# Attention in groups of three units, with wider own maxima, a third q/k set and one sum step per pair, in a fused attention and two-expert-layer kernel

## The chip, the cores and the metric

The kernel runs on one core of one Trainium2 chip. The metric is the device time of one execution in microseconds (us), median of three runs. Engines are named as in the profile: PE (TensorE matmuls), PEld (weight loads of TensorE), DVE (VectorE), ACT (ScalarE), POOL (GpSimd), SP (the queue that issues the DMAs).

## The reference

Three layers in a row, all in float32. q, k and v are (4, 8, 1152, 64), so there are 32 heads.

```python
q_pool = q.reshape(B, H, S // 2, 2, D).mean(axis=3)      # 576 queries per head
scores = (q_pool @ k^T) / 8;  scores -= max over keys
attn   = exp(scores) / (sum over keys + 1e-9);  x = attn @ v   # to (2304, 512)
h = x @ w_in;  g = where(h > 0, h, exp(min(h, 0)) - 1);  x = g @ w_out   # d_ff 2048
logits = x @ phi;  d = softmax over tokens;  c = softmax over 32 slots
slots  = d^T x;  each of 8 experts: relu(slots @ w1[e]) @ w2[e];  out = c @ slot_out
```

## The kernel before

**Who orders the work.** Every step is given to `Plan.add` with a due time, an engine (or a choice of engines) and a duration. `Plan.run` plays the list through once with those durations, latencies (`lat`), a price for a change of TensorE's tiling (`SWITCH`, `HYST`) and priorities (`PRI`, `BIAS`, `LOOK`), and writes the instructions of each engine in the order that comes out. On the chip every engine works through its own list in that fixed order and waits on semaphores. Steps of the attention on TensorE (`fixed=True`) keep the order of their due times.

**Attention (phase 0).** Heads go in 16 pairs, the two heads of a pair side by side in 64 rows each. A pair has 18 units: two halves of 288 queries by nine blocks of 128 keys. A unit (`step`) is: `qk` on TensorE (L688), eight matmuls in 64-row tiles (mode "R") that give the scores less the row maximum in one of three PSUM tokens `psS` (two banks each); one exponential on ACT (L700) into an E tile in SBUF; `acc`, the running sum of the exponentials over the key blocks, on POOL or DVE (L709); and `pv` (L695), the product with v in 64-column tiles (mode "C") into the PSUM bank `psC[h]` of its half. There are six E tiles. Units go in groups of `GU = 2`: first the two `qk` of a group, then the two `pv` of the group before.

**The maxima.** The maximum over keys is needed before a pair's first exponential, so it is worked out one pair ahead from a single product: 576 queries in five tiles by 1152 keys. Six "own" steps per pair take 384 keys each (`max_unit`: `max_mm` L619 into a `psS` token, `max_red` L628 on DVE). The other cells, 192 keys each, are "carried": each of 18 units has one, written behind its scores in the same token and reduced by DVE after the unit's exponential. `max_end` gathers them per half with a small reduce (L668), a transposing product into `psC[h]` (L664) and two scalings (L672) into `nm`.

**Preparing a pair.** q and k are loaded by SP (L520), q is added in twos (`pool_q`, L562, on DVE or POOL). `prep_q` transposes six blocks (L580) through a `psS` token, `prep_k` transposes six blocks (L603) through a `psS` token and three through `psC[1]`. Each is then split into a rounded high part (ACT, L588 and L610) and a low part (DVE, L589 and L611). There are two sets of these operands, taken in turn.

**The sums.** After the last unit of each half a step of its own (`sums`, L719) adds the 128 partial sums with a product with ones in 64-column tiles; ACT writes it to `SS` (L722). After the second half `norm` sends `SS` through two small DMAs (`memf<-memf`) to 18 rows, DVE takes the reciprocal (L744), a DMA writes it to DRAM (`rscr`), two more spread it over the partitions, and a product (L749) gives x.

**After the attention.** The weights of the first expert layer are decoded on DVE during both phases (32 pieces, `decode`, L494 to L506). The layer itself (phase 1) is 32 slots of 48 matmuls for h (L856) and 48 for the output (L895); its first slots are mixed with the last pair of the attention. The last layer (phase 2) streams w1 and w2.

Of the kernel before, what the change touches and what calls it, by code (L numbers as in the profile page):

```python
# [8 lines left out]
F32 = mybir.dt.float32  # L9
# [38 lines left out]
SWITCH = 0.18  # L48


class Plan:
# [57 lines left out]
    def lat(self, a, b):  # L109
        if a == b:  # L110
            return 0.0 if a in ("PE", "SP") else 0.09
        if a == "PE":
            return 0.24
        if b == "PE":
            return 0.27 if a == "ACT" else 0.25
        return 0.16
# [135 lines left out]
PRI = {'1AtaPE': -5.3608, '1LTDVE': -0.4594, '1RTDVE': -7.6429, '2SO*': -0.4526, '1MSACT': -0.9307, '1DN*': 8.8491, '2DNACT': 0.2194, '1wph*': -4.7823, '2BePE': -2.9011, '2erSP': -2.9653, '1EmACT': 4.7478, '1wih*': -3.2155, '1SIDVE': -16.5066, '2yqSP': 2.4557, '1Llg*': -8.1331, '2GPool': 3.2101, '2GDVE': -7.1, '2CDVE': 4.4865, '1PH*': 6.0485, '1xn*': -2.6051, '2SELDVE': 3.5395, '2MDVE': -0.6846, '1xl*': 0.61, '1scroSP': 1.1261, '1DRDVE': -0.4279, '2SOP*': -4.7028, '1xnDVE': 0.4531, '2SIZDVE': 6.7579, '1PHDVE': -0.095, '1Lm*': 5.0157, '2zqSP': -4.2858, '2BsitPE': -5.2295, '1BlgPE': 2.9402, '1X*': -1.2546, '2BsoPE': -9.6495, '1BtaPE': 4.0529, '1MSDVE': -5.9118, '2SODVE': 2.4582, '1wil*': -1.2109, '2AePE': -1.6771, '2SIZPool': -1.8218, '2CPE': 0.3788, 'PMXDVE': 5.8326, '0zSP': 5.8562, '0phiSP': 2.4789, '0UA*': -0.3377, 'PnmACT': 7.2492, '0ONERPool': 2.0662, '0qhACT': 0.8522, '0TMPDVE': -0.5015, 'PKRSP': 2.8555, '0QRSP': 2.4444, 'PMZDVE': 0.1661, '0khACT': 3.538, '0RAWACT': -0.5107, '0ACC*': 1.3624, 'PNQDVE': -2.7745, '0SMSP': 1.1984, '0rscrSP': -1.2373, '0scriSP': -4.5893, '0RBSP': 3.284, 'PqhACT': -3.9283, '0NQ*': 0.8442, '0qlDVE': -4.8402, '0KRSP': -0.8079, '0EAACT': 1.6723, 'PkhACT': 4.0482, '0nmACT': 1.1685, '1AhPE': -5.4283, '1wjh*': -0.2497, '1xh*': -9.449, '1woh*': -13.1407, '1wjl*': 1.9459, '1Hlg*': 1.9084, '1Hm*': -1.551, '1XN*': 1.3572, '1scriSP': -0.3405, '1SI*': 5.0824, '1AoPE': -3.7062, '1LT*': -1.0977}  # L252
BIAS = [{'DVE': 2.6845, 'Pool': 1.8955, 'ACT': -0.4027}, {'DVE': -3.2955, 'Pool': 5.8552, 'ACT': -4.78}, {'DVE': 7.9625, 'Pool': 25.9664, 'ACT': 7.8882}, {'ACT': -14.3311, 'Pool': 2.7731, 'DVE': -2.1432}]
LOOK = {'PE': 0.0215, 'ACT': 0.293, 'DVE': 0.1477, 'Pool': 0.3598, 'SP': 5.2367}
STEP = 1.47
GU = 2
NDEC = [0, 0, 0, 0, 1, 0, 1, 1, 0, 0, 0, 0, 1, 0, 0, 1]
DECS = 0.7438
# [4 lines left out]
TM2 = [-14.582, 27.792, 22.6349, 17.3721]  # L263
TDT = [0.625, 1.728, 6.6355, 1.2]
WARM = [24]
OFF = {'wi': -10.8492, 'wo': 0.9719, 'h': -0.5713, 'o': -0.4908}
EP = 1.3
SLOT = 14.8061
EAV = [26.8636, 30.7913, 35.1115]
OGRP = [[2, 6, 12, 18], [6, 12, 16, 18]]  # L270
DQ = [-10, 0.61]
DK = [[-9, 0.3], [-9, 0.3]]
UC = -14
MAX1 = [[-2, 0.4], [-2, 1.3], [0, -0.1], [0, 0.9], [1, -0.1], [1, 1.3]]
# [12 lines left out]
def attention_moe_softmoe(  # L287
# [20 lines left out]
    MW, NM = 192, S // 192  # L308
# [40 lines left out]
    plan.rot["EA"] = plan.rot["E"] + plan.rot["U"]  # L349
# [7 lines left out]
    def bank(tok):  # L357
# [7 lines left out]
    BASE = {"r": 0, "f": 100000, "y": 200000, "z": 300000, "v": 400000}  # L365
    y_es, z_es = ctx.enter_context(ExitStack()), ctx.enter_context(ExitStack())
# [48 lines left out]
    MZ = carve("v", "MZ", 1, len(NT5) * D)[0].rearrange("p (a j m) -> p a j m", j=2, m=D // 2)
# [113 lines left out]
    for i in range(2):  # L529
        nc.gpsimd.memset(r32(qkb["nm", i]), 0.0)  # L530
# [856 lines left out]
```

## Time and profile before

| what | value |
|---|---|
| runs | 991.01, 995.22, 989.75 us; median 991.01 us |
| profiled execution | span 990.1 us from first to last instruction (no time of it is given beside the span; the median of the runs is 0.9 us above) |
| PE busy | 955.2 us (96%) |
| DVE, ACT, POOL busy | 757.0, 497.7, 396.2 us |
| mean granted TensorE clock | 0.980 |

A busy PE is a modelled figure: matmuls are pipelined, so the starts of the instructions, and not their lengths, tell how fast PE advances. Times in the rows are us from the span's start. fp32 matmuls show as two records each, so one `pv` (two matmuls) is four records of L695, a `qk` is eight of L688 (fp32r).

### The profile page before, as it was taken

The numbers are of one execution on the slowest core, as the hardware profiler recorded it, in microseconds if no ns is written. First come the engines' busy times: TensorE is split into PE (matmuls) and PEld (weight loads), VectorE is DVE, ScalarE is ACT, GpSimd is POOL, SyncE is SP. The second block draws the span as 40 slices with busy tenths as digits, with TensorE's granted clock in tenths as the row PEclk, the third lists the DMA queues.
The fourth block names the chain that finished last, engine by engine and source line by source line (L and its number), as shares of the span: only waits on it lengthen the run. The fifth ranks groups of instructions, "written<-read, shape, count | busy, mean of one in ns | idle before, by whom it ended". The sixth has DMA issues, their size and how long they took to land.

```text
span 990.1 us, 20893 instructions
## 1 busy us (share of the span) xinstructions
PE 955.2 (96%) x8474; PEld 782.5 (79%) x8474; DVE 757.0 (76%) x1278; ACT 497.7 (50%) x891; POOL 396.2 (40%) x278
## 2 busy tenths in 40 slices
PE   7999999999999999999999999999999999999885
PEld 4777767676777677677899999999999999998343
DVE  6677788888777778899998989998866877766213
ACT  2556566555665556565664444444434376442213
POOL 2878889798878878887400000000000000001000
PEclk7999999999999999999999999999999999999897
DMA  7133424224334322221263333333423023233999
GB/s 177 45 86 85 106 74 122 67 78 119 86 85 117 74 73 75 63 72 34 65 219 113 117 95 131 106 98 110 157 86 107 32 97 107 65 107 109 402 362 317
DMA packets 103663, 114.86 MB, mean 116 GB/s; under 512 B 43664, under 2 KB 74896, under 8 KB 103568
## 3 DMA queue, kind: packets, MB, share of 16 engines
q1 hardware_dynamic: 103568, 113.55, 37.7%
q8 instruction: 66, 1.08, 0.5%
q14 instruction: 29, 0.24, 0.1%
HBM read 100.27 MB, written 13.18 MB: 115 GB/s over the span
## 4 chain that ended last, share of the span: by engine, by line
PE 85%; DVE 8%; DMA 3%; ACT 1%; issue 1%; SPq 0%; ACTq 0%; DVEq 0%
PE psC L895 20%; PE psA L856 20%; PE psC L695 13%; PE psA L688 10%; PE psS L688 5%; PE psA L619 3%; PE psS L619 2%; DVE memf L628 2%; DMA memzq<-in_moe_w_dram 2%; PE psA L1241 2%; PE psC L719 1%; PE psA L603 1%; DMA memf<-memf 1%; PE psA L580 1%; PE psC L664 1%; PE psC L1277 1%
## 5 line engine op out<-in xcount | busy, mean ns | idle before, releaser
L709 POOL TENSOR_TENSOR memf<-memf 128x576 f32<-128x576 f32 x241 | 359.8, 1495 | 65.0 <-ACT memf L700 38.6
L895 PE MATMUL psC<-memz 128*128 128x288 f32 x1512 | 224.6, 296 | 1.2 <-DVE memf L906 0.7
L895 PEld LDWEIGHTS psC<-memz 128*128 128x128 f32 x1512 | 208.1, 188 | 4.6 <-ACT memf L514 1.6
L695 PE MATMUL psC<-memf 128*64 128x288 f32 x1152 | 174.6, 420 | 0.0
L700 ACT ACTIVATE memf<-psA 128x576 f32<-128x576 f32 x206 | 132.8, 651 | 66.8 <-PE psA L619 57.7
L628 DVE TENSOR_REDUCE memf<-psA 128x2 f32<-128x384 f32 (+3 forms) x235 | 142.4, 617 | 28.7 <-PE psA L619 13.9
L1347 POOL MEMSET memf<- 128x2048 f32 x1 | 1.8, 1817 | 387.8 <-DVE memz L517 387.8
L906 DVE TENSOR_TENSOR memf<-psC,memf 128x288 f32<-128x288 f32 x220 | 100.3, 462 | 47.4 <-PE psC L895 45.6
L628 DVE TENSOR_REDUCE memf<-psS 128x4 f32<-128x768 f32 (+1 forms) x140 | 103.5, 739 | 38.1 <-PE psS L619 21.2
L514 ACT CAST memz<-memf 128x576 fp32r<-128x576 f32 (+1 forms) x94 | 69.2, 749 | 82.6 <-PE psC L895 42.1
L695 PEld LDWEIGHTS psC<-memf 128*64 128x64 f32 x1152 | 70.0, 136 | 48.9 <-issue 9.9
L517 DVE TENSOR_TENSOR memz<-memf,memz 128x576 fp32r<-128x576 f32 (+1 forms) x108 | 96.9, 906 | 9.8 <-ACT memz L514 8.6
L856 PE MATMUL psA<-memz 128*128 128x288 f32 x512 | 93.8, 295 | 0.0
L867 ACT ACTIVATE memf<-psA 128x576 f32<-128x576 f32 x64 | 41.7, 652 | 103.3 <-PE psA L856 103.2
L688 PE MATMUL psA<-memr 64*128 64x288 f32 x816 | 73.3, 303 | 3.9 <-DVE memf L628 3.9
L856 PEld LDWEIGHTS psA<-memz 128*128 128x128 f32 x512 | 76.6, 188 | 0.0
L700 ACT ACTIVATE memf<-psS 128x576 f32<-128x576 f32 x82 | 53.4, 651 | 41.0 <-PE psS L619 36.1
L688 PEld LDWEIGHTS psA<-memr 64*128 64x128 f32 x816 | 60.1, 188 | 11.0 <-DVE memf L628 6.1
L688 PE MATMUL psA<-memy 64*128 64x288 f32 x624 | 61.3, 301 | 0.5 <-DVE memf L628 0.4
L856 PE MATMUL psA<-memz,memv 128*128 128x288 f32 x256 | 51.9, 296 | 0.0
L688 PEld LDWEIGHTS psA<-memy 64*128 64x128 f32 x624 | 47.3, 187 | 4.5 <-issue 3.5
L870 DVE SCALAR_TENSOR_TENSOR memf<-memf,psA 128x576 f32<-128x576 f32 x64 | 47.6, 744 | 1.7 <-ACT memf L868 1.6
(210 smaller groups left out, 1512.6 us busy)
## 6 DMA issues: line engine op xcount, KB each, us to landing
memf<-wscr SPq DMA_DIRECT2D x32, 512.0 KB
memzq<-in_moe_w_dram SPq DMA_DIRECT2D x30, 512.0 KB
memf<-in_moe_w_dram SPq DMA_DIRECT2D x26, 512.0 KB
memz<-in_q_dram SPq DMA_DIRECT2D x32, 288.0 KB
memz<-in_k_dram SPq DMA_DIRECT2D x32, 288.0 KB
memf<-in_v_dram SPq DMA_DIRECT2D x16, 576.0 KB
memf<-in_moe_w_in_dram SPq DMA_DIRECT2D x32, 256.0 KB
wscr<-memf SPq DMA_DIRECT2D x32, 256.0 KB
```

The costliest lines, as they stand in the source:

```text
L514: return lambda e: nc.scalar.copy(out_, in_) if e == "ACT" else nc.vector.tensor_copy(out_, in_)
L517: return lambda e: ENG[e].tensor_tensor(out_, a, b, ALU.subtract)
L619: nc.tensor.matmul(tile_[:m, j, lo : lo + n * MW], lhsT=qkb["qh", i][js, o : o + m], rhs=qkb["kh", i][js, g * MW : (g + n) * MW], start=Tr ...
L628: add(t, "DVE", dve(2 * n * MW), lambda: nc.vector.reduce_max(MX[i][:m, a, :, g : g + n], v4(got(psS, tok)[:m, :, lo : lo + n * MW], n), a ...
L688: nc.tensor.matmul(sp[:, j, :NH], lhsT=qkb[w, i][js, cs] if w else ONER[js], rhs=qkb[m, i][js, hs], start=(x == 0), stop=(x == 3))
L695: nc.tensor.matmul(psC[h][j * D : (j + 1) * D, :NH], lhsT=VR[i][:, j, c], rhs=e[:, j], start=(c == 0), stop=(c == NC - 1))
L700: add(t + 0.01, "ACT", act(NQ, True), lambda: nc.scalar.activation(got(EAf, E_), got(psS, S_)[:, :, :NH], AF.Exp, scale=1.0 / 16.0), r=[S_ ...
L709: ENG[e].tensor_tensor(ac, a, got(EAf, E_), ALU.add)
L856: nc.tensor.matmul(ph[:, t, :NH], lhsT=a, rhs=x, start=(i == 0), stop=(i == 3 * KD - 1))
L870: add(t + 1.2, "DVE", dve(NQ), lambda: nc.vector.scalar_tensor_tensor(got(Ef, uk), got(Uf, ek), -1.0, ph(), ALU.add, ALU.max), r=[ek, A], ...
L895: nc.tensor.matmul(po_(), lhsT=a, rhs=x, start=(i == 0), stop=(i == 3 * GF - 1))
L906: add(t0 + 0.8, "DVE", dve(NH), lambda: nc.vector.tensor_tensor(d, po_(), d, ALU.add), r=[ck], w=XK)
```

## The change

- Pair 0 keeps groups of two; pairs 1 to 15 go in six groups of three (`GS`). `LAG = 1`: only the last unit of a group has its `pv` in the next group's section; the `pv` of the others come in the group's own.
- Own maxima take 512 keys (six a pair, as before), and 13 carried cells of 212, 214 or 128 keys stand in place of 18 of 192. `CU` says which units carry: the second and third of each group, and unit 15.
- A third set of q/k operands (`qs(p)` in place of `p % 2`), and two KR tiles. From pair 1 on `part` transposes k in three pieces and q in two, all through `psC` in place of `psS`, almost two pairs ahead.
- One `sums` step a pair, with four products in 32-column tiles (two halves by two heads), one `SS` of 288 in place of 576 columns, four small DMAs to 36 rows in place of two to 18, and the reciprocal over 32 columns in place of 64. A third `ACC`.
- Eleven E tiles in place of six (`NEX = 5` more).
- The planner's durations and latencies of DVE and POOL, `SWITCH`, and the tables of priorities and due times are new. The attention's decodes go to other pairs (`NDEC`, six in place of five). q, k and the q sums are due at other times (`LQ`, `LK`, `LN`).

```diff
 def dve(n):
-    return n / 960 + 0.145
+    return n / 960 + 0.07
...
-    return n * 0.00229 + 0.11
+    return n * 0.00229 + 0.17
...
-SWITCH = 0.18
+SWITCH = 0.225
...
-            return 0.0 if a in ("PE", "SP") else 0.09
+            return 0.0 if a in ("PE", "SP") else 0.15 if a == "DVE" else 0.09
...
-GU = 2
-NDEC = [0, 0, 0, 0, 1, 0, 1, 1, 0, 0, 0, 0, 1, 0, 0, 1]
-DECS = 0.7438
+GS = [[2, 2, 2, 2, 2, 2, 2, 2, 2], [3, 3, 3, 3, 3, 3]]
+LAG = 1
+NDEC = [0, -1, 0, 0, 1, 0, -1, 1, 0, 1, 0, 0, 1, 0, 1, 1]
+DECS = 0.5808
...
-SLOT = 14.8061
+SLOT = 12.4951
...
+LQ = [-14.7, -13.9452, -17, -18]
+LK = [-16.5, -17.8646, -18, -22]
+CU = [1, 2, 4, 5, 7, 8, 10, 11, 13, 14, 16, 17, 15]
+PARTS = [..., ..., [['k', 0, -10, -0.1, 1], ['k', 1, -10, 1.7978, 1], ['k', 2, -9, 1.5042, 0], ['q', 0, -8, 1.5, 0], ['q', 1, -7, 1.6969, 0]]]
+MAX2 = [[-6, 1.6], [-5, 1.6], [-4, 1.5272], [-3, 1.6], [-2, 1.6], [-1, 1.6]]
...
-    plan.rot["EA"] = plan.rot["E"] + plan.rot["U"]
+    plan.rot["EA"] = plan.rot["E"] + plan.rot["U"] + [(f"EX{i}",) for i in range(NEX)]
...
+    def part(p, n, g, t, bk):
+        i = qs(p)
+        tok, own_ = ("C", bk), (f"piece{n}{g}", p)
+        m, w = (QC // 2, QP) if n == "q" else (NC // 3, P)
+        def tr():
+            for x in range(m):
+                src = NQt[:w, m * g + x] if n == "q" else KR[p % 2][:, m * g + x]
+                nc.tensor.transpose(psC[bk][:, x * w : (x + 1) * w], src.rearrange("p j d -> p (j d)"), ident[:w, :w])
+        ps = psC[bk][:, : m * w]
+        add(t, "PE", m * (0.092 if n == "k" else 0.08), tr, ...)
+        add(t + 0.01, "ACT", act(m * w, True), lambda: nc.scalar.copy(hi, ps), ...)
+        add(t + 0.02, "DVE", dve(m * w), lambda: nc.vector.tensor_tensor(lo, ps, r32(hi), ALU.subtract), ...)
...
+            whole = [(a, 0, 512, 0, 2) for a in range(5)] + [(4, 512, 512, 2, 2)]
+            part_ = [(a, lo, n, e, 1) for lo, n, e in ((512, 212, 2), (724, 214, 3), (938, 214, 4)) for a in range(3)]
+            part_ += [(3, 512, 212, 2, 1), (3, 724, 214, 3, 1), (3, 938, 214, 4, 1), (4, 1024, 128, 4, 1)]
...
-        t2 = TG(p, u // GU + 1, TC + 0.2 * (u % GU))
+        g2 = g + (k >= gs(p)[g] - LAG)
+        t2 = TP(p, g2, 0.2 * (k - (gs(p)[g] if g2 > g else 0)) + 0.2 * LAG)
...
-                for j in range(2):
-                    nc.tensor.matmul(psC[h][j * D : (j + 1) * D, :NH], lhsT=ONEF, rhs=ac[:, j], start=True, stop=True)
+                    for j in range(2):
+                        for x in range(2):
+                            o = (2 * j + x) * D // 2
+                            nc.tensor.matmul(psC[1][o : o + D // 2, :NH], lhsT=ONEF[:, : D // 2], rhs=accs[x][0][:, j], start=True, stop=True)
...
-        for j in range(2):
-            dma(t, SM[i][j * NC : (j + 1) * NC], SS[j * D : j * D + 1]..., [("SS", 0, 0), ("SS", 0, 1)], [("SM", i, j)], 5e3)
-        add(t + 2, "DVE", 0.55, lambda: nc.vector.reciprocal(rs, sm), ...)
+        for j in range(4):
+            dma(t, SM[i][j * NC : (j + 1) * NC], SS[j * D // 2 : j * D // 2 + 1]..., [("SS", 0)], [("SM", i, j)], 2.5e3)
+        add(t + 2, "DVE", 0.35, lambda: nc.vector.reciprocal(rs, sm), ...)
```

## Rows read from the trace of the kernel before

**Rows 1.** Stages: PE, PEld, DVE, ACT, POOL busy (count), clock, DMA share, GB/s.
```profile
57.02:452.00 394.98, 389.23 (x4089) 278.07 (x4087) 317.91 (x491) 236.41 (x415) 337.20 (x228) 1.00 0.33 84
...
502.87:897.99 395.12, 395.12 (x2965) 390.29 (x2965) 324.32 (x593) 182.54 (x309) 1.54 (x1) 1.00 0.32 105
...
897.99:990.10 92.11, 73.32 (x612) 40.03 (x612) 27.32 (x79) 21.56 (x67) 2.70 (x2) 0.88 0.89 314
```

**Rows 2.** Same view, two of the attention's pairs, between their last sum steps.
```profile
310.35:337.94 27.59, 27.59 (x295) 19.88 (x293) 22.41 (x37) 16.52 (x29) 23.56 (x17) 1.00 0.42 104
...
337.94:369.00 31.06, 29.39 (x295) 21.11 (x293) 21.64 (x37) 16.56 (x29) 23.31 (x17) 0.95 0.33 75
```

**Rows 3.** Timeline of PE inside one pair: start, duration, line, operands, count.
```profile
319.50 0.44 PE L619 MATMUL psS<-memr 64*128 64x384 f32 x2
...
319.78 0.58 PE L688 MATMUL psA<-memy 64*128 64x288 f32 x6
...
320.42 0.58 PE L688 MATMUL psA<-memy 64*128 64x288 f32 x6
...
321.15 1.19 PE L695 MATMUL psC<-memf 128*64 128x288 f32 x8
...
322.27 0.66 PE L688 MATMUL psS<-memy 64*128 64x288 f32 x6
...
322.90 0.25 PE L619 MATMUL psS<-memr 64*128 64x192 f32 x2
...
322.99 0.58 PE L688 MATMUL psA<-memy 64*128 64x288 f32 x6
...
323.72 0.71 PE L695 MATMUL psC<-memf 128*64 128x288 f32 x4
...
324.26 0.66 PE L719 MATMUL psC<-memf 128*64 128x288 f32 x4
...
324.74 0.66 PE L695 MATMUL psC<-memf 128*64 128x288 f32 x4
...
325.33 0.44 PE L619 MATMUL psA<-memr 64*128 64x384 f32 x2
```

**Rows 4.** Chain of waits near the transposes of one pair: start, length, what.
```profile
275.53 0.65 PE psA L580 x6
...
278.76 0.80 PE psA L603 x6
...
279.56 0.33 PE psC L603 x3
```

**Rows 5.** Chain of waits in the last stage, a matmul in four column groups.
```profile
926.42 15.71 PE psA L1241 x128
```

**Rows 6.** Timeline of DVE: two reduces, and a reciprocal that waited.
```profile
310.27 0.54 DVE L628 TENSOR_REDUCE memf<-psA 64x2 f32<-64x384 f32 x1
...
312.06 0.96 DVE L628 TENSOR_REDUCE memf<-psS 128x4 f32<-128x768 f32 x1 [0.43 <-PE psS L619]
...
345.42 0.54 DVE L744 RECIPROCAL memf<-memf 18x64 f32<-18x64 f32 x1 [2.41 <-DMA memf<-memf]
```

**Rows 7.** Waits of DVE from 28 to 452 us: total, times, longest.
```profile
DVE memf L744 <- DMA memf<-memf: 4.5, 3, 2.4
```

**Rows 8.** Timeline of the SP queue's DMA issues in pair 11.
```profile
335.57 2.73 SPq L520 DMA_DIRECT2D memz<-in_k_dram  x2
...
339.08 2.65 SPq L520 DMA_DIRECT2D memf<-memf  x2
```

**Rows 9.** Lines L709 and L562 by engine: min/median/max ns, first and last start.
```profile
L709 POOL TENSOR_TENSOR memf<-memf x241: 1395/1417/2296, 24.8 to 480.3; 128x576 f32<-128x576 f32 x121
...
L709 DVE TENSOR_TENSOR memf<-memf x15: 744/748/1980, 127.4 to 466.7; 128x576 f32<-128x576 f32 x15
...
L562 DVE TENSOR_TENSOR memf<-memz x13: 944/1452/2168, 5.4 to 390.5; 96x768 f32<-96x768 f32 x13
```

**Rows 10.** Costliest groups of the page: the exponential of a unit.
```profile
L700 ACT ACTIVATE memf<-psA 128x576 f32<-128x576 f32 x206 | 132.8, 651 | 66.8 <-PE psA L619 57.7
```

More of the change, by code (lines that the diff above doesn't have):

```diff
@@ L114, in lat @@
         if b == "PE":
-            return 0.27 if a == "ACT" else 0.25
-        return 0.16
+            return 0.27 if a == "ACT" else 0.32 if a == "DVE" else 0.25
+        return 0.235 if a == "DVE" else 0.16
     def run(self):
@@ L527, in attention_moe_softmoe @@
     nc.gpsimd.memset(MX[1], 0.0)
-    for i in range(2):
+    for i in (1, 0, 2):
         nc.gpsimd.memset(r32(qkb["nm", i]), 0.0)
@@ L618, in max_mm, with max_red @@
             js = slice(j * D, (j + 1) * D)
[L619 removed]
+            nc.tensor.matmul(tile_[:m, j, at : at + n], lhsT=qkb["qh", i][js, o : o + m], rhs=qkb["kh", i][js, lo : lo + n],
                              start=True, stop=True)
[L622 to L625 removed]
+    def max_red(tok, p, cell, at, t, behind=()):
@@ L626, in max_red @@
         i = p % 2
+        a, _, n, e, ne = cell
         m = QT[a][1]
-        add(t, "DVE", dve(2 * n * MW), lambda: nc.vector.reduce_max(
-            MX[i][:m, a, :, g : g + n], v4(got(psS, tok)[:m, :, lo : lo + n * MW], n), axis=AX.X), r=[tok, *behind], w=[("MX", i, a, g)])
-    def max_deps(p, g, n):
-        return [("qh", p % 2)] + [("kh", p % 2, x) for x in sorted({g // 4, (g + n - 1) // 4})]
-    def max_unit(p, a, g, t):
-        tok = ("S", "max", p, a, g)
-        add(t, "PE", 0.172, lambda: max_mm(got(psS, tok), p, a, g, 2, 0), r=max_deps(p, g, 2), w=[tok], mode="R", fixed=True)
-        max_red(tok, p, a, g, 2, 0, t + 0.01)
@@ L639, in attention_moe_softmoe, with max_deps @@
-    carry, own = {}, {}
+        add(t, "DVE", dve(2 * n), lambda: nc.vector.reduce_max(
+            MX[i][:m, a, :, e : e + ne], got(psS, tok)[:m, :, at : at + n].rearrange("p j (g k) -> p j g k", g=ne), axis=AX.X),
+            r=[tok, *behind], w=[("MX", p, a, e)])
+    def max_deps(p, cell):
+        a, lo, n = cell[:3]
+        qx, kx = ((0,), (0,), (0, 1), (1,), (1,))[a], range(lo // 384, (lo + n - 1) // 384 + 1)
+        return [("qh", qs(p), x) for x in qx] + [("kh", qs(p), x) for x in kx] + [("now", "qh", p, x) for x in qx] + [("now", "kh", p, x) for x in kx]
@@ L640, in attention_moe_softmoe, with max_unit @@
+    def max_unit(p, cell, t):
+        tok = ("S", "max", p, *cell[:2])
+        add(t, "PE", 0.012 + cell[2] / 2400, lambda: max_mm(got(psS, tok), p, cell, 0), r=max_deps(p, cell), w=[tok], mode="R", fixed=True)
+        max_red(tok, p, cell, 0, t + 0.01)
+    carry, own, cells_of = {}, {}, {}
     for p in range(NP):
-        own[p] = []
-        cells = {h: [(a, g) for a in ((0, 1, 2), (3, 4))[h] for g in range(0, NM, 2)] for h in range(2)}
         if p == 0:
-            own[p] = [(a, g, *((-7 + x // 2, 0.2 * (x % 2)) if GU == 2 else (-5 + x // 3, 0.2 * (x % 3)))) for x, (a, g) in enumerate(cells[0])]
-            own[p] += [(a, g, *MAX1[x]) for x, (a, g) in enumerate(cells[1])]
-            continue
@@ L647, in attention_moe_softmoe @@
-        for h in range(2):
-            nown = (4, 2)[h]
-            own[p] += [(a, g, *MAX2[h][x]) for x, (a, g) in enumerate(cells[h][:nown])]
-            units = [u for u in range(UC, UC + 18)][10 * h : 10 + 8 * h]
-            rest = sorted(((a, g + y) for a, g in cells[h][nown:] for y in range(2)), key=lambda x: x[1] // 4)
-            for u, x in zip(units, rest, strict=True):
-                carry[(p - (u < 0), u % NU)] = (p, *x)
-    cells_of = {(p, a, g) for p in own for a, g, *_ in own[p]} | set(carry.values())
+            whole = [(a, 384 * x, 384, 2 * x, 2 - x // 2) for a in range(5) for x in range(3)]
@@ L656, in max_end @@
+        cells_of[p] = {c[:1] + c[3:4] for c in whole + part_}
     def max_end(p, h, t):
@@ L687, in qk @@
                     js = slice(j * D, (j + 1) * D)
-                    nc.tensor.matmul(sp[:, j, :NH], lhsT=qkb[w, i][js, cs] if w else ONER[js], rhs=qkb[m, i][js, hs], start=(x == 0), stop=(x == 3))
+                    nc.tensor.matmul(sp[:, j, :NH], lhsT=qkb[w, s][js, cs] if w else ONER[js], rhs=qkb[m, s][js, hs], start=(x == 0), stop=(x == 3))
             if more:
-                max_mm(sp, *more, 1, NH)
+                max_mm(sp, *more, NH)
         def pv():
@@ L702, in step @@
         if more:
[L703 to L705 removed]
+            max_red(S_, *more, NH, t + 0.02, [("SX", p, u)])
+        ac, ak = acc_of(p, h)
         if c:
```

219 lines of the change are left out of this document (136 added, 83 removed).

## The prediction

> **What bounds the kernel now.** I read the windows by stage first. Attention from pair 1 to pair 14 takes 394.98 us (14 periods of 28.21), the expert layer 395.12 with PE busy throughout, and the end 92.11, where the DMA share is 0.89 [rows 1]. The change touches instructions of the first of these only. In the others it moves due times, and a stage whose PE never rests, or which streams weights, cannot give much. So the question is a period of the attention.
>
> Next the same view for single pairs. The least period is 27.59 us, with PE busy for all of it; the longest, pair 11, is 31.06 with 1.67 us of PE idle and a clock of 0.95 [rows 2]. The mean of 28.21 is thus 0.62 above the least, 8.7 us over 14 pairs. POOL is busy 337.20 of 394.98 us, DVE 317.91 [rows 1]: neither sets the period, but both are close.
>
> Then the timeline of PE in that least pair, starts only [rows 3]. A two-unit group without extras goes from the start of its `pv` at 321.15 to the first `qk` at 322.27 (1.12), the second at 322.99 (0.72) and the next `pv` at 323.72 (0.73): 2.57 us, nine times per pair. Within a section, steps follow one another more closely: a `qk` after another in the same tiling starts 0.64 later (319.78 to 320.42), and a product in 64-column tiles after another 0.48 later (324.26 to 324.74). Two `qk` and two `pv` at those spacings would be 2.24, so the two changes of tiling in a group cost 0.33.
>
> **The change, part by part.** All per pair of the kind 1 to 14, against 27.59.
>
> *Groups of three.* A third unit adds one `qk` and one `pv` inside the sections: 2.57 + 0.64 + 0.48 = 3.69. Six such groups are 22.14, nine of two are 23.13: -0.99 [rows 3].
>
> *One sum step.* The first goes: -0.48, the spacing of one L719 step [rows 3]. The step that stays has four products in 32-column tiles. Its nearest row is the last stage's four-wide product: 16 sets of four products of 512 columns take 15.71 us, 0.98 each [rows 5]; scaled to 288 columns 0.55. So its price lies between 0.48 and 0.55, far from the 0.96 of products that do not overlap. I take 0.48.
>
> *Maxima.* A carried cell of 192 keys costs 0.09 (322.90 to 322.99). An own step costs (321.15 - 319.50) - (323.72 - 322.27) = 0.20 [rows 3]. Before: 18 x 0.09 + 6 x 0.20 = 2.82. The 192 keys more of an own step cost 0.11; at that rate 512 keys cost 0.27, 213 keys 0.10 and 128 keys 0.05, so 12 x 0.10 + 0.05 + 6 x 0.27 = 2.87. If own steps cost only their share of the 0.09 per 192 keys, 0.26, it is 2.81. I take no change; the total of keys is the same.
>
> *Transposes in pieces.* Before, q costs 0.65, k 0.80 + 0.33 in adjoining steps [rows 4]. With b for a block of 96 columns, 4b/3 for one of 128 and a for entering the tiling, a + 6b = 0.65 and a + 12b = 1.13 give b = 0.08, a = 0.17. Five separate pieces are 5 x 0.17 + 0.48 + 0.96 = 2.29 against 1.78: +0.51. If two adjoin, +0.34; if the one placed before a `pv` section pays a change of tiling of its own as well (half of 0.33), +0.68. I take 0.51. ACT and DVE get two more instructions each, beside PE's work.
>
> *Together.* -0.99 - 0.48 + 0.51 = -0.96: a least period of 26.63. Fourteen pairs give -13.4. Pair 15 prepares nothing after it: -0.99 - 0.48 = -1.5. Pair 0 keeps its groups; it loses one sum and gains some pieces: -0.3. Sum -15.2.
>
> *Stalls.* One part of the 8.7 us has a cause I can see. In pair 11 the reciprocal stood 2.41 us at the head of DVE for its DMA [rows 6], with the reduces behind it and PE behind them. DVE waited so three times, 4.5 us in all [rows 7]. SP had issued two k loads (2.73 us) just ahead of the two sum loads, and those took 2.65 to issue [rows 8]. The new `LK` puts the k loads some 11 units earlier, for which the second KR tile gives room. That can give back those 4.5 us of DVE and the 3.5 us by which pair 11 exceeds the least period. Against it, four sum loads have to be issued where there were two. The reciprocal waits for the last; at half of 2.65 per issue the two more add 2.65. The plan books 0.63 for each (`dma`), so it expects 1.26 of this; what is missing, 1.4 us or, where issues are as quick as booked, nothing, DVE waits at the reciprocal. Of that PE sees what exceeds the slack of the reduces. I let the two cancel, with the decodes (six in place of five among these pairs) counted in: the stalls stay at about 8.7 us.
>
> *Free by cover.* Eleven E tiles and the third set add no instruction. They loosen waits: an exponential need not wait for POOL's `acc`, and a set is not overwritten while its pair runs. If POOL falls behind there are five units more before ACT must stop. Without that cover each late `acc` would hold an exponential.
>
> Forecast: 990.1 - 15.2 = 974.9 us of span. The page gives no time beside the span; the median lies 0.9 above, so 975.8.
>
> **The rivals.**
>
> *A, the forecast.* 975.8; its own range, from the transposes (14 x 0.17 = 2.4 each way) and half of the stalls, is 969 to 983.
>
> *B, the stalls go too.* Early k loads, more E tiles and the third set take the 8.7 us away: 967.1; with pieces that adjoin (14 x 0.17) 964.7. For it: pair 11 alone holds 3.5. Against it: four sum loads.
>
> *C, POOL and DVE together become the bound.* An `acc` takes at least 1.395 us on POOL and 0.744 on DVE, but up to 1.98 there; `pool_q` on DVE takes 0.944 at best, 1.452 in the median [rows 9]. So such instructions hold each other up. If what POOL and DVE read in SBUF with two operands goes one at a time, a pair needs 17 products on POOL (16 `acc` and x) at 337.20 / 228 = 1.48 [rows 1] plus one `pool_q` of 1.45, together 26.6. That is all of the new period, with the decodes on top. An `acc` given to DVE relieves POOL by 1.48 and costs DVE 0.75. If that comes in front of a reduce in two pairs of three, 14 x 0.5 = 7 us are lost: 983. For it: the medians above the minima. Against it: pairs at 27.59 run without any PE idle with 23.56 of POOL and 22.41 of DVE.
>
> The Trainium skill, SBUF — State Buffer, section "Who interferes with whom", says that a DVE instruction with two SBUF inputs and a GpSimd instruction that reads SBUF exclude each other for a whole instruction. By that rule the sum would be that of C, 983, and not 975.8. The trace agrees so far: `pool_q` on DVE at 1.452 where 0.944 is possible.
>
> *D, slower: the PSUM tokens.* There are three `psS` tokens and now four uses in a group: three units and an own step. Reduces of 384 and 768 elements take 0.54 and 0.96 [rows 6], so 0.42 per 384; a carried cell (about 426 elements) takes 0.59 and an own one (1024) 1.24. With exponentials of 0.65 [rows 10] one behind another, the third of them (its `qk` done at 0.63 + 0.64 + 0.73 = 2.0, then a semaphore) ends about 2.9 us after the group's first `qk`, and the last reduce at about 4.7 (2.9 + 0.59 + 1.24, own one last). The third `qk` of the next group, which takes that token, starts at 3.69 + 0.27 + 0.63 + 0.64 = 5.2. The margin is 0.5, less the two semaphores between. An `acc` (0.75) or `pool_q` (1.45) ahead of those reduces uses it up, and the reduce, the `qk` and the next exponential wait in turn. From 0.16 us a group (0.96 / 6) the gain is gone. If 45 of the 90 groups lose 0.55, that is 25 us: 1001. For it: DVE's queue is in order, and a single late reciprocal cost pair 11 3.5 us. Against it: two-unit groups have no idle at 81% DVE, and 22.4 of 26.6 is 84%.
>
> The Trainium skill, TensorEngine Tiling (Array Packing), section "Performance Considerations", warns that tiled matmuls leave the evacuation of PSUM as the bottleneck. By that rule D decides, at 1001; the trace does not show it reached yet, since PE has no idle at 27.59 [rows 2].
>
> *E, no gain.* The 0.33 per group belongs to the first matmul after a wait and stays with every unit: only -0.48 + 0.51 is left, 990 to 991.
>
> **How the numbers follow.** Chances: A 0.55, B 0.17, C 0.13, D 0.10, E 0.05. The predicted time is A's, 975.8 us. The range goes from 963 (B with 2 us more from the start) to 988 (C with the dearer pieces, 983 + 2.4, and a little more); D, E and the edges of the others, some 2 in 10, lie outside. Half a per cent, 5 us, is about what a measurement can tell here, so faster is below 986: A, B and most of C, 0.82. Within: the rest of C and E, 0.08. Slower: D, 0.10.
>
> **What would show it.** Right: a least period between last sum steps near 26.6; starts of 1.6 us for a section of three `pv` and about 2.0 for three `qk`; one L719 step of 0.48 a pair; transposes of 0.4 to 0.5 in five places; k loads well ahead of the sum loads; the expert slots at the pace that they have now. Wrong: PE waiting for L628 in most groups (D), DVE's two-operand instructions above 1.4 us and periods of 27.4 (C), periods still near 28 with sections of three that take half as long again as those of two (E). The chief step that can fail is the one on stalls, which I set equal and did not derive.

## The result and the profile after

The changed kernel takes 967.42 us (median of four runs, 965.89 to 968.13) against 990.38 for the kernel before beside it; the ratio is 0.9766, with a 95% interval of 0.9733 to 0.9799. Forecast were 975.8 us and a range of 963 to 988, with 0.82 on a gain. The profiled execution took 967.65 us, with a span of 965.9 (before: 990.1). Times here and below are medians of the fast runs; one run of experiment 6 (3069.7 us) and one of experiment 8 (5080.3 us) are left out.

The page's busy times and its chain of what ended last:

```profile
PE 936.7 (97%) x8324; PEld 766.8 (79%) x8324; DVE 760.2 (79%) x1312; ACT 483.7 (50%) x882; POOL 307.3 (32%) x223
...
PE 92%; DVE 4%; DMA 2%; ACT 1%; POOL 1%; issue 0%; ACTq 0%; POOLq 0%; DVEq 0%
```

PE is nearly the whole of the chain. POOL does 55 instructions and 89 us less than before: more of the `acc` are on DVE, which yet is hardly busier (757.0 us before).

The same view as in [rows 1] and [rows 2]: pairs 1 to 14 between the last sum steps (L792 now), the last 395.12 us of the experts, the last stage, then pairs 9, 13 and 14, and the stretch from the last sum step of pair 14 to the last expert product:

```profile
57.60:432.56 374.96, 372.80 (x3940) 261.88 (x3938) 328.32 (x497) 235.77 (x428) 270.32 (x185) 1.00 0.34 90
487.44:882.56 395.12, 395.12 (x2974) 390.71 (x2973) 314.04 (x598) 170.15 (x286) 2.76 (x2) 1.00 0.29 95
882.56:965.90 83.34, 63.73 (x540) 31.36 (x538) 22.21 (x66) 20.20 (x63) 0.00 (x0) 0.84 0.98 347
271.57:298.30 26.73, 26.73 (x285) 18.84 (x284) 23.69 (x36) 16.50 (x31) 20.04 (x14) 1.00 0.41 107
378.84:407.46 28.62, 27.30 (x287) 18.83 (x285) 27.61 (x43) 19.30 (x36) 16.52 (x11) 1.00 0.16 51
407.46:432.56 25.10, 24.46 (x261) 16.76 (x259) 22.00 (x35) 15.11 (x27) 18.51 (x11) 1.00 0.21 66
432.56:882.56 450.00, 448.98 (x3416) 437.72 (x3417) 366.08 (x685) 201.44 (x342) 9.21 (x6) 1.00 0.30 100
```

The windows of [rows 1] for the experts and the end meet at 897.99, but the last expert product of the kernel before ended at 908.71. From there, and from its last sum step of pair 14, the kernel before shows:

```profile
452.00:908.71 456.71, 453.57 (x3435) 439.72 (x3432) 379.39 (x668) 214.96 (x367) 27.93 (x18) 1.00 0.30 101
908.71:990.10 81.39, 63.32 (x540) 30.27 (x538) 20.15 (x63) 21.35 (x66) 0.00 (x0) 0.86 1.00 355
```

Three things are to be seen. The attention's 14 pairs lost 20.0 us (394.98 to 374.96). The least period fell from 27.59 to 26.73. And the stalls fell: pairs 1 to 13 exceeded 13 least periods by 8.7 us before, and now by 349.85 (57.60 to 407.45) - 13 x 26.73 = 2.4. Eleven of these periods are 26.73 to 26.78, pair 12 takes 27.0, and only pair 13 stands out, where DVE is busy for 27.61 of 28.62 us. Pair 14 is no fair measure of a stall: neither kernel transposes anything in it (the pieces, L667, are 2.57 us of PE's busy time in pair 13 and none in pair 14), and so its 25.10 lie below the least period of the others. In the kernel before it took 27.59 all the same, with 1.04 us of PE idle (0.64 now).

PE inside a pair, starts only, as in [rows 3]:

```profile
271.23 0.40 PE L682 MATMUL psS<-memy 64*128 64x512 f32 x2
271.56 0.43 PE L792 MATMUL psC<-memf 128*32 128x288 f32 x1
...
272.18 0.71 PE L765 MATMUL psC<-memf 128*64 128x288 f32 x4
...
273.78 1.32 PE L758 MATMUL psA<-memr 64*128 64x288 f32 x16
...
276.49 0.71 PE L765 MATMUL psC<-ex,memf 128*64 128x288 f32 x4
277.02 1.14 PE L765 MATMUL psC<-memf 128*64 128x288 f32 x8
278.09 0.55 PE L667 MATMUL psC<-ident,memz 128*128 128x128 f32 x3
278.57 0.80 PE L758 MATMUL psA<-memr 64*128 64x288 f32 x8
```

Three `pv` take 1.60 us (272.18 to 273.78, 276.49 to 278.09), as forecast. A section that opens with the sum step takes 2.22 (271.56 to 273.78), so that step costs 0.62. A piece of k is 0.48 (278.09 to 278.57); one of q is 0.40 in the same view.

DMA issues of SP around one pair's sums, as in [rows 8]:

```profile
326.27 3.11 SPq L544 DMA_DIRECT2D memf<-memf  x4
...
336.53 1.31 SPq L544 DMA_DIRECT2D memz<-in_k_dram  x2
...
353.00 3.10 SPq L544 DMA_DIRECT2D memf<-memf  x4
```

The k loads stand 16 us ahead of the sum loads, and four sum loads take 3.10 to issue where two had taken 2.65. DVE, which waited 4.5 us in three places for this DMA [rows 7], waits once for 0.3.

**The ledger of the span** (-24.2 us): the first pair +0.6; pairs 1 to 14 -20.0, of it 13 x 0.86 = 11.2 from the least period, 6.3 from stalls in pairs 1 to 13 and 2.5 in pair 14; from the last sum step of pair 14 to the last expert product -6.7 (456.71 to 450.00, of which PE idle 3.14 to 1.02); the last stage +1.9 (81.39 to 83.34), with a DMA share of 1.00 before and 0.98 now. The experts keep their pace: 2974 matmuls in their last 395.12 us, 2965 in the equally long window of [rows 1].

### The profile page after: what moved, and what is told of

The parts are those of the page before. It is cut to its first block, busy times and chain, and to the rows that moved or that the text cites. A ratio compares the mean times of both kernels' runs of the same rounds, so it can differ in the third digit from the quotient of the medians.

```text
span 965.9 us, 20539 instructions
## 1 busy us (share of the span) xinstructions
PE 936.7 (97%) x8324; PEld 766.8 (79%) x8324; DVE 760.2 (79%) x1312; ACT 483.7 (50%) x882; POOL 307.3 (32%) x223
## 4 chain that ended last, share of the span: by engine, by line
PE 92%; DVE 4%; DMA 2%; ACT 1%; POOL 1%; issue 0%; ACTq 0%; POOLq 0%; DVEq 0%
PE psC L971 21%; PE psA L932 21%; PE psC L765 15%; PE psA L758 11%; PE psS L758 6%; PE psC L667 3%; PE psA L682 3%; DMA memzq<-in_moe_w_dram 2%; PE psA L1317 2%; DVE memf L689 2%; PE psS L682 1%; PE psC L792 1%; PE psC L727 1%; PE psC L1353 1%; PE psB L1123 1%; POOL acc L778 1%
## 5 line engine op out<-in xcount | busy, mean ns | idle before, releaser
L689 DVE TENSOR_REDUCE memf<-psA 128x2 f32<-128x428 f32 (+5 forms) x205 | 156.6, 787 | 15.1 <-ACT ex L770 7.2
L778 POOL TENSOR_TENSOR memf<-memf 128x576 f32<-128x576 f32 x76 | 111.7, 1470 | 47.0 <-DVE memf L778 26.0
L765 PE MATMUL psC<-memf 128*64 128x288 f32 x632 | 99.6, 417 | 0.0
L943 ACT ACTIVATE memf<-psA 128x576 f32<-128x576 f32 x64 | 41.8, 654 | 114.2 <-PE psA L932 114.2
L932 PE MATMUL psA<-memz 128*128 128x288 f32 x512 | 94.0, 295 | 0.0
L689 DVE TENSOR_REDUCE memf<-psS 128x2 f32<-128x428 f32 (+3 forms) x95 | 75.3, 792 | 10.0 <-ACT memf L770 5.0
L765 PE MATMUL psC<-ex,memf 128*64 128x288 f32 x520 | 80.9, 414 | 0.7 <-DVE memr L674 0.7
L770 ACT ACTIVATE memf<-psA 128x576 f32<-128x576 f32 x101 | 65.6, 652 | 31.1 <-PE psA L758 21.6
L932 PEld LDWEIGHTS psA<-memz 128*128 128x128 f32 x512 | 76.7, 188 | 0.1
L778 POOL TENSOR_TENSOR memf<-memf,ex 128x576 f32<-128x576 f32 x44 | 64.1, 1457 | 30.9 <-DVE memf L778 23.1
L770 ACT ACTIVATE ex<-psA 128x576 f32<-128x576 f32 x87 | 56.7, 652 | 22.3 <-PE psA L758 17.4
L765 PEld LDWEIGHTS psC<-ex,memf 128*64 128x64 f32 x520 | 33.8, 136 | 26.2 <-issue 6.8
L932 PE MATMUL psA<-memz,memv 128*128 128x288 f32 x256 | 51.8, 295 | 1.0 <-DVE memf L946 1.0
L778 POOL TENSOR_TENSOR acc<-acc,memf 128x576 f32<-128x576 f32 x29 | 42.6, 1470 | 19.1 <-DVE acc L778 16.2
```

The lines of the kernel that those rows point to most:

```text
L689: add(t, "DVE", dve(2 * n), lambda: nc.vector.reduce_max(MX[i][:m, a, :, e : e + ne], got(psS, tok)[:m, :, at : at + n].rearrange("p j (g ...
L765: nc.tensor.matmul(psC[h][j * D : (j + 1) * D, :NH], lhsT=VR[i][:, j, c], rhs=e[:, j], start=(c == 0), stop=(c == NC - 1))
L770: add(t + 0.01, "ACT", act(NQ, True), lambda: nc.scalar.activation(got(EAf, E_), got(psS, S_)[:, :, :NH], AF.Exp, scale=1.0 / 16.0), r=[S_ ...
L778: ENG[e].tensor_tensor(ac, a, got(EAf, E_), ALU.add)
L932: nc.tensor.matmul(ph[:, t, :NH], lhsT=a, rhs=x, start=(i == 0), stop=(i == 3 * KD - 1))
L943: add(t, "ACT", act(NQ, True), lambda: nc.scalar.activation(got(Ef, uk), ph(), AF.Relu, scale=-1.0), r=[A], w=[uk])
```

## The experiments

Twelve kernels ran. Each time stands against runs of the kernel before on the same chip (989.6 to 991.4 us); intervals are 95%. "Excess" is pairs 1 to 13 less 13 least periods, as above (8.7 before, 2.4 after).

**1. The change without its groups of three.** Groups of two for all pairs; the places of pieces and own maxima were set by hand for nine groups.

```diff
-GS = [[2, 2, 2, 2, 2, 2, 2, 2, 2], [3, 3, 3, 3, 3, 3]]
+GS = [[2, 2, 2, 2, 2, 2, 2, 2, 2], [2, 2, 2, 2, 2, 2, 2, 2, 2]]
```

> The changed kernel with groups of two in all pairs (nine a pair), all else kept. If a group of three saves two changes of tiling in three units (0.33 us each group, the forecast's first term), the least period rises from 26.74 by 0.99 to about 27.7, and the time from 967.4 to about 982. If the groups do nothing, the period stays at 26.7 and the time at 967.

988.25 us, ratio 0.997 (0.9956 to 0.9985). Ten steady periods, and all 14 pairs:

```profile
84.66:361.48 276.82, 276.69 (x2833) 185.99 (x2831) 228.19 (x349) 166.64 (x309) 216.13 (x152) 1.00 0.37 101
56.97:444.06 387.09, 385.80 (x3944) 258.87 (x3942) 322.38 (x490) 233.25 (x431) 294.99 (x207) 1.00 0.33 91
```

The period is 27.68 in the mean, 0.93 more than the 26.75 of the change's first ten pairs, where 0.99 was forecast. But there is hardly any PE idle: these 14 pairs, in groups of two, are 7.9 us shorter than before at a least period (27.65) that is no shorter, and the excess is 1.5. So the stalls went with the rest of the change, and groups of three brought the other 12.1 (387.09 to 374.96). The whole is slow since the stretch after pair 14 lost 10.6 us (444.06 to the end at 988.0, 543.9 us; 533.3 after). The due times of that hand-over to the experts were fitted to threes, which is the likely cause and was not tried apart.

**2. Groups of three in the kernel before**, nothing else, the due places shifted to six groups.

```diff
-GU = 2
+GU = 3
-DK = [[-9, 0.3], [-9, 0.3]]
+DK = [[-6, 0.9], [-6, 0.9]]
```

> The kernel before with groups of three and nothing else of the change: six E tiles, a carried cell in every unit, transposes through the PSUM tokens, two sums a pair. Forecast's first term: least period 27.59 - 0.99 = 26.6, time 991 - 15 = 976. Theory of the PSUM tokens (rival D): three units and an own step on three tokens, with a carried cell in each unit, make TensorE wait for the reduces in most groups; the period is then 28 or more and the time 991 or more.

1028.4 us, ratio 1.0371 (1.0337 to 1.0405); 14 pairs take 427.20 us, with 32.8 of PE idle, and the least period is 29.1. The chain of waits at a transpose of k:

```profile
113.30 0.82 PE psS L603 x6
...
114.14 0.81 ACT memy L610
...
114.97 1.42 DVE memy L611 x2
116.39 0.88 DVE memf L628
...
117.31 0.80 PE psA L688 x8
```

The transpose holds a token for its ACT and DVE passes; DVE then owes a reduce, and the next `qk` starts 3.2 us after the transpose ended. With threes, transposes through `psS` and a carried cell on every unit, PE is idle for 1.4 us or more in every pair. That is rival D's mechanism, at more than the price forecast for it.

**3. Six E tiles in place of eleven.**

```diff
-NM, NEX = 5, 5
+NM, NEX = 5, 0
```

> The changed kernel with six E tiles in place of eleven. If the five more tiles are what took the stalls of 0.6 us a pair away, exponentials wait for accumulations again and the time rises from 967.4 by 5 to 9 us, to about 975. If they only cover a backlog that does not arise, it stays within 2 us of 967.

968.88 us, ratio 0.9786 (0.9758 to 0.9813); the 14 pairs take 375.83 (374.96 after), with pairs 1 and 5 at 27.40 and 27.23. The extra tiles are worth about 1.5 us in the medians, which the intervals do not tell from nothing: cover that was hardly needed.

**4. The k and q loads at their old due times.**

```diff
-LQ = [-14.7, -13.9452, -17, -18]
-LK = [-16.5, -17.8646, -18, -22]
+LQ = [-14.7, -13.9452, -19.5, -19.5]
+LK = [-16.5, -17.8646, -16.5, -16.5]
```

> The changed kernel with the loads of q and k from pair 2 on due where they were before (39 and 33 units ahead), so that the k loads stand just ahead of the sum loads in the SP queue. If the place of the k loads was the cause of the late reciprocal, DVE waits for it 1 to 2.4 us in several pairs again and the time rises by 3 to 5 us, to about 971. If not, 967 within 1.

967.95 us, ratio 0.9771 (0.9752 to 0.979). It tells nothing on the question: the due times changed no engine's order of work, nor that of SP's list. It is a repeat of the change, and shows how well one repeats (0.5 us).

**5. Whole transposes through `psS`** again, from pair 3 on.

```diff
+        elif p > 2:
+            for g in range(2):
+                prep_k(p, g, TP(p, -10, 1.7 + 0.01 * g))
+            prep_q(p, TP(p, -8, 1.5))
```

> The changed kernel, but from pair 3 on q (six blocks) and the first six blocks of k are transposed whole through a PSUM token psS, as before, and the last three of k through psC; times in the plan as for the pieces. By the price of the pieces (0.51 us a pair more than whole) it would gain 13 x 0.5 = 6.6 us: 961. By the theory that groups of three only work because the transposes left the three tokens (a token held through copy and subtraction, some 2 us, makes the reduces and the scores wait), each pair loses 1 to 3 us net: 980 to 1000, with TensorE waiting around L622 and L647.

981.29 us, ratio 0.99 (0.9878 to 0.9922). A least pair, and all 14 pairs up to the same point as in the change:

```profile
277.62:304.49 26.87, 26.68 (x286) 18.91 (x284) 23.70 (x35) 16.54 (x30) 21.40 (x16) 1.00 0.38 109
57.98:445.90 387.92, 373.84 (x3939) 263.69 (x3937) 336.66 (x477) 229.21 (x402) 290.99 (x195) 0.99 0.33 89
```

Who PE waited for from 28 to 450 us (us in total, times, longest):

```profile
PE psC L792 <- POOL acc L778: 4.2, 1, 4.2
PE psA L758 <- DVE memf L689: 4.2, 5, 2.5
```

The 14 pairs take 13.0 us more than in the change, with 14.1 us of PE idle in place of 2.2. Of it 4.2 are one wait of pair 14's sum step for an `acc` on POOL, which is no matter of tokens; the next in size are waits for DVE's reduces of a token. The excess is 9.9. By starts the pieces cost PE 0.46 a pair (3 x 0.48 + 2 x 0.40 = 2.24 against the 1.78 of [rows 4]). In the periods that price does not show: with whole transposes the least one is 26.87, 0.14 longer than with pieces, since PE waits about 0.2 us in it for the subtraction of L655 and is busy for only 0.05 less (26.68).

**6. Carried cells on the first and second unit of each group** in place of the second and third.

```diff
-CU = [1, 2, 4, 5, 7, 8, 10, 11, 13, 14, 16, 17, 15]
+CU = [0, 1, 3, 4, 6, 7, 9, 10, 12, 13, 15, 16, 17]
```

> The changed kernel with the carried cells on the first and second unit of each group in place of the second and third. The own step at the end of the section needs the first unit's token. If that token's reduce is then late (the forecast's rival of the PSUM tokens), each group loses 0.4 to 0.5 us: least period 29 to 30, time about 1000. If the tokens have slack, period and time stay at 26.7 and 967.

1019.88 us, ratio 1.0297 (1.0271 to 1.0324): the same work takes 52 us more. Waits of PE in pairs 1 to 14:

```profile
PE psA L682 <- DVE memf L689: 22.8, 61, 2.5
PE psS L682 <- DVE memf L689: 9.1, 20, 1.5
```

One group in the chain of waits:

```profile
91.91 0.73 PE psS L758 x8
92.64 0.12 PE psS L682 x2
...
92.84 0.66 ACT ex L770
...
93.53 0.62 DVE memf L689
...
94.19 0.49 PE psS L682 x2
```

The own maximum (94.19) needs the token of the group's first unit. Where that unit carries nothing, its token is free after the exponential (93.50); here the reduce of the carried cell comes in between, and PE stands. The 84 groups of pairs 1 to 14 lose (423.69 - 374.96) / 84 = 0.58 us each, of which 0.36 is PE idle (32.6 us in place of 2.2) and the rest slower starts after it. In the change the own step of such a group starts about 0.4 us after the first unit's exponential has ended (88.47, after 88.1), so a reduce of 0.62 in between does not fit. The forecast's margin of 0.5 us was worked out for the third token and not for this one; this run does not measure it, but it shows that which unit carries decides whether a margin of that size is kept.

**7. Two sum steps**, with two loads and a reciprocal over 64 columns, as before.

```diff
-            if h:
-                t3 = TP(p, g2 + SUMD[0], SUMD[1])
+            t3 = TP(p, g2 + SUMD[0], SUMD[1])
...
-        for j in range(4):
+        for j in range(2):
```

> The changed kernel with the two sum steps, the two sum loads and the 64-wide reciprocal of before. The forecast's term: one step of 0.48 us more a pair, least period 27.2, time 967.4 + 7.7 = 975. If the second step is hidden or the four loads cost as much as it saves, the time stays near 967.

981.33 us, ratio 0.9899 (0.9879 to 0.9918). The least period is 27.07 (+0.34; 0.48 was forecast), and the excess is 8.5. The 14 pairs take 384.33, 9.4 more than in the change: 4.8 (14 x 0.34) by the least period, the rest with 5.4 us of PE idle in place of 2.2 and a fall of the granted clock to 0.50 from 412.5 to 415.9, behind a wait of 1.88 us. The change has no such fall in its pairs.

**8. The kernel before with its reciprocal placed late**: the planner is told a higher price for the sum loads and so lists the reciprocal later on DVE; the copy of `SEL` was given a later due time as well.

```diff
-[("SS", 0, 0), ("SS", 0, 1)], [("SM", i, j)], 5e3)
+[("SS", 0, 0), ("SS", 0, 1)], [("SM", i, j)], 400e3)
-        add(t + 2, "DVE", 0.6, sel,
+        add(t + 20, "DVE", 0.6, sel,
```

> The kernel before with two edits to the plan alone: it books 1.5 us more for each sum load, so that the reciprocal stands later in DVE's list, and the small selection step at the end (L1340, L1342) is due 18 us later, away from the memset of POOL. If the stalls of 990 us come from these two places, 4.6 and about 4 us go: 982. If they move to other places, 990.

992.58 us, ratio 1.0022 (1.0006 to 1.0038). DVE no longer waits for the sums' DMA, and pair 11 takes 27.84 in place of 31.06. But other pairs grew in the new order (pair 4 from 27.64 to 29.17, pair 10 from 27.59 to 28.86): the 14 pairs take 392.78, only 2.2 less, the excess is 6.5, and the gain is lost again by the end.

**9. The change with the planner's old durations and latencies.** Same structure, another order.

```diff
-    return n / 960 + 0.07
+    return n / 960 + 0.145
...
-SWITCH = 0.225
+SWITCH = 0.18
...
-            return 0.0 if a in ("PE", "SP") else 0.15 if a == "DVE" else 0.09
+            return 0.0 if a in ("PE", "SP") else 0.09
```

> The changed kernel with the planner's durations and latencies of DVE and POOL and its price of a change of tiling as before (0.145 in place of 0.07 us a DVE instruction, DVE's results seen 0.06 to 0.08 us sooner, SWITCH 0.18); the order of instructions on all engines follows from them. If the stalls went because the plan now books what DVE really does, they come back: least period 26.7 as now, but some pairs 0.5 to 1.5 us longer, time 972 to 980. If the order does not depend on it, 967.

1018.33 us, ratio 1.0269 (1.0249 to 1.0289). Early pairs still take 26.75 to 27.5; pairs 7 to 13 take 28 to 33, and pairs 1 to 13 are 26.5 us longer than in the change (376.33 against 349.85). Pair 14's 44.46 are no stall in the main: 96 matmuls of the experts (L932) come into it, where the change has none. The rest of the loss falls behind pair 13 and was not followed. Who PE waited for up to 450 us, the first lines:

```profile
PE psC L667 <- DVE memy L674: 5.7, 2, 2.9
PE psC L667 <- DVE memr L674: 5.7, 2, 2.9
```

The chain of waits in one such place:

```profile
160.62 0.68 DVE memf L530
161.31 2.10 DVE memf L586
163.40 2.15 DVE memf L689 x3
...
165.60 0.80 PE psA L758 x8
```

A decode (L530) and `pool_q` (L586) stand in DVE's list ahead of reduces and of a piece's subtraction that PE needs sooner.

**10. The k loads of a later pair directly ahead of the four sum loads** in SP's list.

```diff
         for j in range(4):
+            k_ahead(p + 4, j, t)
             dma(t, SM[i][j * NC : (j + 1) * NC], SS[...]
...
-        load_k(p, T(p, LK[min(p, 3)], 0))
+        if p < 4:
+            load_k(p, T(p, LK[min(p, 3)], 0))
```

> The changed kernel with the two k loads (of the pair four further on) put directly ahead of the four sum loads in the SP queue, all needed much later than they land. If k loads just ahead of the sum loads made the reciprocal late in the kernel before, DVE waits for it 1 us or more in several pairs and the pairs lengthen; time 970 to 975. If not, 967 within 1.

980.51 us, ratio 0.9882 (0.9843 to 0.9922), where 970 to 975 or 967 was expected. Pairs 1 to 11 keep 26.76 on average. SP around one pair's sums, and DVE's wait for the sums' DMA from 28 to 452 us (L823 is the reciprocal here):

```profile
244.28 3.00 SPq L544 DMA_DIRECT2D memz<-in_k_dram  x2
247.38 3.10 SPq L544 DMA_DIRECT2D memf<-memf  x4
```

```profile
DVE memf L823 <- DMA memf<-memf: 2.4, 5, 1.0
```

The k loads stand directly ahead of the sum loads again, as in [rows 8], and DVE waits for these five times, 2.4 us in all (0.3 in the change). That is so although the planner, which counts the k loads, puts the reciprocal later in DVE's list: where it does not wait it starts 7.2 us after the sum step, against 6.0 in the change and 5.0 before. So k loads ahead do make the reciprocal wait, and so does an early place in the list. TensorE loses nothing by these five waits, since no pair up to pair 11 is longer. The loss falls in pairs 12 to 15 and at the hand-over; its cause was not followed.

**11. The kernel before, one POOL memset moved** behind the copy of `SEL`, for a stall of the last expert slot.

```diff
-lambda: nc.gpsimd.memset(G, 0.0), r=[("elu", 0), ("elu", 1)], w=[("G", 0)])
+lambda: nc.gpsimd.memset(G, 0.0), r=[("elu", 0), ("elu", 1), ("SEL", 0)], w=[("G", 0)])
```

> The kernel before with POOL's memset of G (L1347, 1.8 us) made to wait for the selection copies of DVE (L1342), so that the two cannot overlap. If the memset is what held the copy for 2.18 us and, through DVE's list, TensorE for about 4 us in the last slot, that slot ends 4 us sooner; the time falls to 986 if the last stage follows it, and stays at 990 if the streaming of the weights sets its end anyway.

990.89 us, ratio 0.9998 (0.9986 to 1.0009). The copies still took 2.18 us: both memsets overlap them as they did, so the edit did not part them and the run tells nothing on them.

**12. The kernel before with the planner's new durations and latencies**, the reverse of experiment 9.

```diff
-    return n / 960 + 0.145
+    return n / 960 + 0.07
...
-SWITCH = 0.18
+SWITCH = 0.225
...
-            return 0.0 if a in ("PE", "SP") else 0.09
+            return 0.0 if a in ("PE", "SP") else 0.15 if a == "DVE" else 0.09
```

> The kernel before, its structure unchanged (groups of two, transposes through psS, two sum steps, six E tiles), with only the planner's new durations and latencies of DVE and POOL and the new SWITCH, which here are a change of the order of instructions and of nothing else. Theory: the durations and latencies that match the chip are what takes the stalls of the attention away, so the 8.7 us over pairs 1 to 14 fall to 1 or 2 us, the least period stays at 27.5 to 27.6, and the whole comes to 983 to 986 us. Rival: the new durations only pay together with the new structure (pieces out of psS, carried cells on the second and third unit, loads of k earlier, due times placed for them); the stalls here stay or move, and the time is 990 us or more, with the least period still near 27.6.

1007.72 us, ratio 1.0152 (1.0124 to 1.018). The windows of 14 pairs:

```profile
58.09:457.33 399.24, 390.50 (x4090) 278.20 (x4088) 339.53 (x542) 238.27 (x419) 289.50 (x196) 1.00 0.34 87
```

The wait of DVE for the sums' DMA from 28 to 470 us:

```profile
DVE memf L744 <- DMA memf<-memf: 9.2, 8, 3.7
```

The rival holds: in the old structure, with its old due times, the new durations do not remove the stalls, the 14 pairs take 4.3 us more, and the reciprocal waits longer than before (9.2 against 4.5).

## Why the prediction was right, and where it was off

*Groups of three: right.* Forecast -0.99 a pair; undone -0.93 (experiment 1). Rival E falls: the 0.33 goes with the number of groups, and so of changes of tiling, and not with the units.

*One sum step: direction right, size off.* -0.48 was forecast with the four-wide step at 0.48, "between 0.48 and 0.55". It costs 0.62 by the starts above, so the gain is 0.96 - 0.62 = 0.34, and undoing it gives 0.34. The 512-column row from which it was scaled had its sets one behind another in one tiling; a single step has not.

*Maxima: right.* 0.10 for a carried cell (271.12 to 271.23 and others), 0.24 for an own one at the end of a section (the chain's 411.97 to 412.21), where 0.10 and 0.27 were forecast.

*Pieces: right by starts, not by periods.* +0.51 forecast, +0.46 by starts. The three, -0.93 - 0.34 + 0.46 = -0.81, come near the measured -0.86; the least period was forecast at 26.63 and is 26.73. But putting whole transposes back gave no shorter period (experiment 5), so no run confirms this term by itself. The forecast also charged it to 14 pairs: pair 14 holds no pieces.

*Stalls: the step that failed.* "The stalls stay at about 8.7 us" was set, not derived, by letting early k loads and four sum loads cancel. They fell to 2.4 in pairs 1 to 13, and neither term decided it. Four loads issue in 3.10 us, 0.45 more than two and not 2.65 more. And taking the reciprocal's wait away mends pair 11 but gives 2.2 us in all (experiment 8), not 4.5. Pair 11's excess of 3.5 us, which the forecast counted as a stall that early k loads take away, was half of it a clock: PE was idle for 1.68 and then ran at half the granted clock from 346.5 to 349.9, which is about 1.7 us more (an estimate, half of 3.4; see the last section).

*The time of rival B, 967.1, was met in part by luck.* B gave back all 8.7 us of stalls; the runs show 6.3. Of the 9.0 us by which the span of 965.9 lies under the forecast's 974.9, about 6.3 are these stalls, 1.5 pair 14 and 5.2 the stretch to the end of the experts. The least period (1.3), the first pair (0.9) and the last stage (1.9) took some back.

What removed the stalls is shown in part. They went without groups of three (experiment 1), and without the extra E tiles (3). Each of these, undone alone, brings waits back: pieces out of `psS` (excess 9.9), one sum step (8.5), carried cells off the first unit (0.58 a group), and the planner's durations with the order that follows from them (pairs 1 to 13 26.5 us longer). The durations alone do not carry over (12). The reading that fits is that tokens are released early enough, and that an order was found in which DVE's reduces and subtractions come when PE needs them. But each of these runs keeps due times and priorities that were fitted to the whole change, so part of a loss can be the misfit and not the part undone, and no single part holds a share that could be named apart. How much the third q/k set or the new priorities do by themselves was not tried, and the early k loads were tried only where the order around them changed too (10).

*Rival D* is real as a mechanism: 0.58 us a group where the first unit carries, and 38 us where threes meet whole transposes and a carried cell on every unit (experiment 2). The change avoids it by the choice of the carrying unit and by the pieces. The Trainium skill, TensorEngine Tiling (Array Packing), section "Performance Considerations", warns that the evacuation of PSUM may become the bottleneck once tiling speeds TensorE up. Those two runs agree with it, and the changed kernel does not show it: there PE waits for DVE's reduces less than 1 us in 14 pairs.

*Rival C* was not reached: POOL is busy 270.32 of 374.96 us. `pool_q` on DVE still takes 1.27 us in the mean where 0.944 is possible, but PE hardly waits for any of it.

*Outside the pairs:* -6.7 us to the end of the experts, where -1.5 was forecast for pair 15. 2.1 of the difference is PE idle that is gone; the rest lies in the mix of pair 15 with the first slots, where experiment 1 lost 10.6 us, and was not taken apart. The last stage gave 1.9 back; it streams weights at a DMA share of 0.98.

## What to carry to other kernels

The saving worked out from starts inside one period held within about a tenth in sum here (0.96 forecast, 0.86 measured), and within a third term by term; the stalls around it are the uncertain term, and deserve their own derivation rather than "as before". When a stage ends without the preparation that its other periods hold, leave that last period out before counting stalls. When more work is put between two changes of tiling, ask which PSUM token the next product needs and what the last reader of that token is; moving a reduce to a unit whose token is needed later was worth more here than the change itself. Durations given to a static planner are part of a kernel: with other ones the same instructions took 51 us longer, and the good ones made another structure slower.

## What the runs showed of the hardware

TensorE paid twice for one long wait. In pair 11 of the kernel before it was idle for 1.68 us until 346.43, behind the reduces that stood behind the late reciprocal. From 346.5 to 349.9 the granted clock was 0.50, the lower of its two levels (1.2 in place of 2.4 GHz), though PE was busy throughout. The two first steps after the wait, and that stretch:

```profile
346.43 1.32 PE L688 MATMUL psA<-memr 64*128 64x288 f32 x8 [1.68 <-DVE memf L628]
...
347.70 1.22 PE L688 MATMUL psA<-memr 64*128 64x288 f32 x8
```

```profile
346.50:349.90 3.40, 3.40 (x24) 2.84 (x26) 1.80 (x4) 1.30 (x2) 1.11 (x1) 0.50 0.14 51
```

These two `qk`, with a carried cell between them, started 1.27 us apart, where such a step takes 0.72 in [rows 3]. In the changed kernel no single wait of PE in these pairs is longer than 0.74 us (at 402.90), and the clock stays at 1.00 through all 14 pairs.

Two copies of 128x32 elements on DVE took 2.18 us together before (2.16 and 2.09, one begun 0.09 after the other). They came beside two POOL memsets of the last stage, and ended 0.05 after the second did (901.99, 901.94). POOL and DVE before, in start and duration:

```profile
899.24 1.82 POOL L1347 MEMSET memf<- 128x2048 f32 x1 [387.79 <-DVE memz L517]
900.99 0.95 POOL L1346 MEMSET memf<- 128x1024 f32 x1
...
899.81 2.18 DVE L1342 COPY memf<-memf 128x32 f32<-128x32 f32 x2
```

In the changed kernel the same copies begin 0.2 us before the first of the same memsets ends:

```profile
872.24 1.81 POOL L1423 MEMSET memf<- 128x2048 f32 x1 [390.98 <-PE psC L971]
...
873.82 0.28 DVE L1418 COPY memf<-memf 128x32 f32<-128x32 f32 x2
873.98 1.01 POOL L1422 MEMSET memf<- 128x1024 f32 x1
```

They end at 874.10, again 0.05 after a memset, the first one (874.05), and took 0.28 us. The Trainium skill, SBUF — State Buffer, section "Who interferes with whom", says that DVE in a two-port mode, which copies can enter, and GpSimd exclude each other for a whole instruction. That copies end just behind a memset in both kernels agrees with it, as far as POOL's spans go, which are rough. Why they waited for the second memset in one and only for the first in the other is open, and no run parted them. PE lost 0.7 us by it before (L895 at 902.07).
